# Mamba-2 scan, then PReLU MLP: reordering the first token group (one weight piece ahead of the PReLUs, others behind, states ahead of the scans, later rows moved)

## Chip, cores, metric

One core of one Trainium2 chip. The metric is the device time of one execution in microseconds (us), median over runs. Most runs of one kernel lie within 0.3% of each other, some sets spread more; ranges are given. TensorE is PE, VectorE is DVE, ScalarE is ACT, GpSimd is POOL.

## The reference, cut to what matters

```python
# x (4,8,768,32), a (4,8,768), B, C (4,8,768,16): a chunked state space scan
for c in range(nc):                               # nc = 24 chunks of 32
    L = np.exp(cum[..., :, None] - cum[..., None, :]) * causal
    M = np.einsum('bhin,bhjn->bhij', Cc, Bc) * L
    y = M @ xc + (Cc @ state) * np.exp(cum)[..., None]
    state = decay_full * state + sum_j(B_j x_j decay_from_j)
# then an MLP with a PReLU that has one slope per hidden unit
h = x @ w_in                                      # (3072,256) @ (256,2048)
g = np.maximum(h, 0) + alpha * np.minimum(h, 0)
out = g @ w_out                                   # (2048,256)
```

The weights arrive as 64-bit floats and are made 32-bit on the chip, in 16 pieces of 512 KB (the inputs `in_moe_w_in` and `in_moe_w_out`).

## The kernel before

Tokens go through in six groups of 512 (four chunks of 128, so two pairs of chunks). The first group has a loop of its own over f, the 16 blocks of 128 hidden units: a hidden product, a PReLU, an output product four blocks behind. Between these run the conversion of the weights and the scan (`ssm`) of pairs 2 and 3, which make the second group's tokens.

A piece is converted in six operations: two on ACT and one on POOL (the first part), two on DVE (sign; shift and combine), and a last addition on POOL. The order in which the program issues instructions matters for what an engine waits for: before, ACT's copy of B and C (37.26 us in the timeline that the prediction shows) stands behind the first part of piece 6, which waited for its load until 36.11.

```python
def convert_a(dst, src, sg):                      # first part of a piece
    nc.scalar.activation(out=t, in_=hi, func=ACTF.Abs, scale=0.125)        # ACT
    nc.gpsimd.tensor_scalar(out=t, in0=t, ..., op0=ALU.min, op1=ALU.max)   # POOL, clamp
    nc.scalar.activation(out=g, in_=half, ...)                             # ACT

def convert_b(dst, src, sg):
    nc.vector.tensor_single_scalar(out=r, in_=hi, scalar=SIGN, ...)        # DVE, L238
    nc.vector.scalar_tensor_tensor(out=r, in0=t, scalar=3, in1=r, ...)     # DVE, L239
# convert() adds on POOL (L261); convert_next(first=True) converts the next piece i
# and then issues the first part of piece i + 2

def pair(gp):                                     # each yield ends a stage; gp = 2, 3 here
    ...                                           # transposes of B and C, copy bc
    if not fine:
        spread_c()                                # ACT: two products cz
    bn = bns.pop(gp) if gp in bns else pair_loads(gp)   # POOL: B scaled
    ...
    yield
    decays(0)                                     # DVE: four scans
    yield
    decays(1)                                     # DVE: four scans
    yield
    states(added(ss_tile()))                      # PE: B's products with x; DVE: state
    c_decayed()
    yield
    gram = products_bc()                          # PE: eight score products; one of their four
                                                  # buffers is a hidden-product buffer (two exist)
    ...                                           # DVE: four multiplications, in two stages
    yield
    ...                                           # PE: y; ACT: copy into the next group's tokens

# driver, first group
convert_a(*pieces[3])
prelus = [hidden_two(0, 0, 2 * Q, spare())]       # second-half hidden products of f = 0, 1
prelus[0]()                                       # their PReLUs on DVE
prelus = [hidden_two(0, 2, 2 * Q, spare())]
convert_a(*pieces[4])
convert_next(first=False)                         # piece 3
prelus[0]()
identity_bank()
convert_a(*pieces[5])
convert_next()                                    # piece 4, and first part of piece 6
in_steps = {8: 0, 10: 1, 12: 2, 14: 3}
for f in range(FIRST, NF):                        # f = 4 .. 15
    if f == 9:
        rows_clamp(1); held["pr"] = rows_scan(1); rows_out(1)    # DVE: "the later rows"
    if f <= 10: ssm(2)
    if f >= 9: ssm(3)
    hidden(0, f)                                  # PE, then ACT and DVE for the PReLU
    convert_next()
    output(f - FIRST)                             # PE
    if f in in_steps:
        weight_sums(wi, in_sums, 0, in_steps[f])  # POOL
```

## Time and profile before

| | before |
|---|---|
| time, median of 4 runs | 378.16 us (378.02 to 378.35) |
| span of the profiled run | 376.5 us |
| PE busy, share of span | 365.5 us, 97% |
| PE waits, 26 to 84 us | 3.9 us, all before 62 us |
| transposes of pair 2 to transposes of pair 4 | 30.73 to 85.41 us: 54.68 us |

The last row is the yardstick of this study. Between these two points PE does the same work in every kernel below, and the start of a run is outside it: transposes of pair 2 begin anywhere from 30.1 to 31.0 us without a difference in the program, so whole times carry that noise. The prediction shows the lines of the waits and the timeline.

### The profile page before, as it was taken

What the parts mean: (1) busy time and instruction counts of PE and PEld (TensorE: products, weight loads), DVE (VectorE), ACT (ScalarE), POOL (GpSimd) and SP (SyncE); (2) the same over time, 40 slices, a digit from 0 to 9 for tenths busy, and PEclk for the clock granted to TensorE, in tenths of its full rate; (3) what the DMA queues carried; (4) which work ended last, traced back from release to release, by engine and by line L of the source; (5) the groups of instructions that cost most, each with busy time, mean ns of one, the idle gap of its engine ahead of it and who ended that gap; (6) DMA issues with size and microseconds to landing.
All of it is one profiled execution on the core that took longest, in us unless ns stands there. A gap on an engine that the chain in (4) does not pass through costs nothing.

```text
span 376.5 us, 6178 instructions
## 1 busy us (share of the span) xinstructions
PE 365.5 (97%) x2223; PEld 294.0 (78%) x2223; DVE 242.2 (64%) x461; ACT 179.8 (48%) x384; POOL 203.7 (54%) x212
## 2 busy tenths in 40 slices
PE   8898899999999999999999999999999999999996
PEld 7675466668778788788788788788788788888884
DVE  7885799967537737747737847647856734543364
ACT  2557666525354445445435535535625525543541
POOL 4875366778766836535455445356364355264512
PEclk9999999999999999999999999999999999999999
DMA  7989798821008801001801801901811000001003
GB/s 141 225 190 304 205 276 178 169 67 57 28 0 182 154 2 57 2 0 30 177 6 36 174 2 29 182 0 28 152 33 22 9 0 15 16 0 30 1 0 84
DMA packets 121878, 30.71 MB, mean 82 GB/s; under 512 B 93736, under 2 KB 117752, under 8 KB 121848
## 3 DMA queue, kind: packets, MB, share of 16 engines
q1 hardware_dynamic: 116736, 29.74, 35.6%
q10 hardware_dynamic: 5112, 0.59, 1.1%
q8 instruction: 17, 0.28, 0.3%
q14 instruction: 13, 0.11, 0.1%
HBM read 26.98 MB, written 3.34 MB: 81 GB/s over the span
## 4 chain that ended last, share of the span: by engine, by line
PE 85%; DVE 5%; DMA 3%; POOL 2%; ACT 2%; issue 1%; ACTq 1%; POOLq 0%; DVEq 0%
PE hp L766 33%; PE bank L741 32%; PE bank L680 5%; PE hp L642 3%; PE ss L623 2%; DMA raw<-in_moe_w_in_dram 2%; PE ss L564 2%; PE ss L616 1%; DVE dec L438 1%; PE ss L519 1%; DMA nat<-in_B_dram 1%; PE hp L657 1%; PE hp L564 1%; PE ss L469 1%; DVE wr L239 1%
## 5 line engine op out<-in xcount | busy, mean ns | idle before, releaser
L809 POOL TENSOR_TENSOR gt<-gt 128x512 f32<-128x512 f32 x58 | 73.7, 1271 | 31.7 <-DVE gt L751 24.8
L751 DVE SCALAR_TENSOR_TENSOR gt<-hp,s_mul,gt 128x256 f32<-128x256 f32 x120 | 52.6, 479 | 47.8 <-ACT gt L749 46.8
L741 PE MATMUL bank<-gt,w_out 128*128 128x256 f32 x320 | 82.5, 382 | 0.4 <-ACT o_sb L687 0.4
L749 ACT ACTIVATE gt<-hp,s_alpha 128x256 f32<-128x256 f32 x120 | 50.4, 471 | 47.1 <-PE hp L766 32.8
L741 PEld LDWEIGHTS bank<-gt,w_out 128*128 128x128 f32 x320 | 60.0, 190 | 11.2 <-issue 2.3
L800 POOL TENSOR_TENSOR gt<-gt 128x512 f32<-128x512 f32 x20 | 25.4, 1271 | 78.1 <-DVE gt L751 78.1
L741 PE MATMUL bank<-gt,ws 128*128 128x256 f32 x240 | 58.3, 379 | 0.0
L741 PEld LDWEIGHTS bank<-gt,ws 128*128 128x128 f32 x240 | 45.1, 190 | 5.8
L438 DVE TENSOR_TENSOR_SCAN dec<-abc,bank 128x256 f32<-128x256 f32 x80 | 48.1, 660 | 0.0
L766 PE MATMUL hp<-xs,w_in 128*128 128x256 f32 x160 | 42.8, 390 | 0.0
L766 PE MATMUL hp<-xT,w_in 128*128 128x256 f32 x160 | 41.9, 384 | 0.0
L766 PE MATMUL hp<-xs,ws 128*128 128x256 f32 x160 | 41.1, 379 | 0.0
L785 DVE TENSOR_TENSOR hp<-hp,u 128x512 f32<-128x512 f32 x20 | 14.0, 700 | 39.6 <-ACT u L783 39.6
L774 ACT COPY m<-hp 128x512 f32<-128x512 f32 x20 | 11.7, 586 | 51.4 <-PE hp L766 51.4
L766 PEld LDWEIGHTS hp<-xs,w_in 128*128 128x128 f32 x160 | 28.7, 189 | 7.7 <-issue 3.3
L766 PEld LDWEIGHTS hp<-xs,ws 128*128 128x128 f32 x160 | 30.4, 190 | 4.1
L766 PEld LDWEIGHTS hp<-xT,w_in 128*128 128x128 f32 x160 | 29.7, 190 | 5.0 <-issue 1.4
L680 PEld LDWEIGHTS bank<-w_out,gt 128*128 128x128 f32 x128 | 24.1, 190 | 11.7 <-issue 4.9
L680 PE MATMUL bank<-w_out,gt 128*128 128x256 f32 x128 | 30.7, 381 | 2.3 <-POOL w_out L261 2.3
L789 DVE TENSOR_TENSOR c<-hp,m 128x512 f32<-128x512 f32 x20 | 13.6, 682 | 19.2 <-PE hp L766 19.2
L642 PE MATMUL hp<-xT,w_in 128*128 128x512 f32 x48 | 23.3, 607 | 0.3 <-DVE gt L646 0.3
L783 ACT COPY u<-hp 128x512 f32<-128x512 f32 x20 | 11.7, 586 | 22.9 <-PE hp L766 22.9
(155 smaller groups left out, 553.7 us busy)
## 6 DMA issues: line engine op xcount, KB each, us to landing
abc<-z SPq DMA_DIRECT2D x20, 512.0 KB, 5.3
raw<-in_moe_w_in_dram SPq DMA_DIRECT2D x8, 512.0 KB, 4.9
raw<-in_moe_w_out_dram SPq DMA_DIRECT2D x8, 512.0 KB, 6.5
xt<-in_x_dram SPq DMA_DIRECT2D x24, 128.0 KB, 3.2
out_dram<-o_sb SPq DMA_DIRECT2D x32, 64.0 KB, 1.9
nat<-in_B_dram SPq DMA_DIRECT2D x22, 64.0 KB, 2.8
nat<-in_C_dram SPq DMA_DIRECT2D x22, 64.0 KB, 3.3
ap<-pf SPq DMA_DIRECT2D x11, 128.0 KB
```

Source lines behind the costliest of these rows:

```text
L438: nc.vector.tensor_tensor_scan(out=dv[:, k, hs], data0=abc[k][:, hs], data1=ident_p[0], initial=0.0, op0=ALU.mult, op1=ALU.add)
L642: nc.tensor.matmul(hp, w_in[:, k, f * P : (f + 1) * P], xts[g][:, k], start=(k == 0), stop=(k == KC - 1))
L680: nc.tensor.matmul(pos[0][t // 2][:, t % 2], gt[:, t * Q : (t + 1) * Q], w_out[:, f], start=(f == 0 and t % 2 == 0), stop=(f == NF - 1), s ...
L741: nc.tensor.matmul(ms[g][i][:, h], w, blocks[g, z][n][:, p], start=(q == 0 and h == 0), stop=(q == NQ - 1), skip_group_check=True)
L749: nc.scalar.mul(o[:, p], h[:, p], s_alpha[:, fs[p]])
L751: nc.vector.scalar_tensor_tensor(out=o[:, p], in0=h[:, p], scalar=s_mul[:, fs[p]], in1=o[:, p], op0=ALU.mult, op1=ALU.max)
L766: nc.tensor.matmul(to[:, p], w(2 * z + p), b, start=start and p == 0, stop=True, skip_group_check=True)
L774: nc.scalar.copy(out=m1, in_=A)
L785: nc.vector.tensor_tensor(out=Y, in0=Y, in1=u2, op=ALU.add)
L789: nc.vector.tensor_tensor(out=c22, in0=A, in1=m5, op=ALU.add)
L800: nc.gpsimd.tensor_tensor(out=tc_, in0=g22, in1=g12, op=ALU.subtract)
L809: eng.tensor_tensor(out=o, in0=x0, in1=x1, op=ALU.subtract)
```

## The change

Its intent is to close PE's gaps in the first group: piece 3 ahead of the PReLUs that wait for ACT, the first parts of pieces 5 and 6 behind the PReLU of f=4, B's scaling for pairs 2 and 3 made sooner, their states ahead of the scans (which saves a stage in each), and the later rows from f=9 to f=11.

```diff
 def pair(gp):
-        if not fine:
+        if gp < 2:
             spread_c()
 ...
         else:
+            if gp > 1:
+                states(added(ss_tile()))
+                c_decayed()
             decays(0)
 ...
             if gp != 1:
                 decays(1)
+            if gp > 1:
+                spread_c()
 ...
-            if not fine:
-                yield
-            states(added(ss_tile()))
-            c_decayed()
+            if fine:
+                states(added(ss_tile()))
+                c_decayed()
             yield
             gram = products_bc()
 # driver
     convert_a(*pieces[3])
-    prelus = [hidden_two(0, 0, 2 * Q, spare())]
-    prelus[0]()
-    prelus = [hidden_two(0, 2, 2 * Q, spare())]
+    convert_next(first=False)
+    hidden_two(0, 0, 2 * Q, spare())()
+    rest = hidden_two(0, 2, 2 * Q, spare())
     convert_a(*pieces[4])
+    rest()
+    identity_bank()
+    bns[2] = pair_loads(2)
     convert_next(first=False)
-    prelus[0]()
-    identity_bank()
-    convert_a(*pieces[5])
-    convert_next()
 ...
-        if f == 9:                      # the later rows
 ...
         hidden(0, f)
-        convert_next()
+        if f < FIRST + 2:
+            convert_a(*pieces[f + 1 + (f > FIRST)])
+        convert_next(first=f > FIRST)
+        if f == FIRST:
+            convert_a(*pieces[6])
+        if f == 8:
+            bns[3] = pair_loads(3)
+        if f == 11:                     # the later rows
```

More of the change, by code (lines that the diff above doesn't have):

```diff
@@ L522, in added @@
             return dps
-        if fine:
-            for k in range(2):
-                for w in range(2):
-                    half_decays(k, w)
-                    if k == 1 and w == 1:
-                        spread_c()
-                    yield
-        else:
-            decays(0)
-            if gp == 1:
-                dps = added(dps)
-            if gp:
-                yield
-            if gp != 1:
-                decays(1)
         def states(dps):
@@ L553, in states @@
             masked[b] = st[-1]
+        if fine:
+            for k in range(2):
+                for w in range(2):
+                    half_decays(k, w)
+                    if k == 1 and w == 1:
+                        spread_c()
+                    yield
+        else:
+            if gp > 1:
+                states(added(ss_tile()))
+                c_decayed()
+            decays(0)
+            if gp == 1:
+                dps = added(dps)
+            if gp:
+                yield
+            if gp != 1:
+                decays(1)
+            if gp > 1:
+                spread_c()
         def products_bc():
@@ L590, in pair @@
         else:
-            if not fine:
-                yield
-            states(added(ss_tile()))
-            c_decayed()
+            if fine:
+                states(added(ss_tile()))
+                c_decayed()
             yield
@@ L976 @@
             load_rows(1)
-        if f == 9:
-            rows_clamp(1)
-            held["pr"] = rows_scan(1)
-            rows_out(1)
         if f <= 10:
@@ L985 @@
         hidden(0, f)
-        convert_next()
+        if f < FIRST + 2:
[6 more added lines that the diff above has]
+        if f == 11:
+            rows_clamp(1)
+            held["pr"] = rows_scan(1)
+            rows_out(1)
         output(f - FIRST)
```

## The prediction

> **What bounds the kernel now.** I read the page first: engine shares, then the 40 slices. The TensorE clock is 9 tenths or more in every slice, so the clock is no issue, and PE is busy almost throughout.
>
> ```profile
> PE 365.5 (97%) x2223; PEld 294.0 (78%) x2223; DVE 242.2 (64%) x461; ACT 179.8 (48%) x384; POOL 203.7 (54%) x212
> PE   8898899999999999999999999999999999999996
> ```
>
> Only the first seven slices (9.4 us each) and the last fall short of 9. So a change in the first group of tokens can only win what PE loses there. The second view is PE's waits, once for 26 to 62 us and once for 62 us to the end:
>
> ```profile
> PE bank L680 <- POOL w_out L261: 2.3, 2, 1.4
> PE ss L564 <- DVE state L547: 0.5, 1, 0.5
> PE bank L616 <- DVE dec L600: 0.5, 1, 0.5
> PE hp L642 <- DVE gt L646: 0.3, 1, 0.3
> PE hp L657 <- ACT xT L630: 0.3, 1, 0.3
> ...
> PE bank L741 <- ACT o_sb L687: 0.4, 1, 0.4
> PE turned L852 <- DVE c L878: 0.3, 1, 0.3
> ```
>
> The first five rows are the early stretch, the last two all the rest: 3.9 us against 0.7. After 61 us the chain that ended last is PE work in unbroken order, so a microsecond won before 61 us should come out at the end, provided no new wait arises. The third view is the timeline of 30 to 60 us:
>
> ```profile
> 31.17 1.89 PE L642 MATMUL hp<-xT,w_in 128*128 128x512 f32 x4
> 33.12 1.33 POOL L261 TENSOR_TENSOR w_out<-wr,wg 128x512 uint32<-128x512 uint32 x1
> 33.42 1.57 DVE L239 SCALAR_TENSOR_TENSOR wr<-wt,wr 128x512 uint32<-128x512 uint32 x1
> 34.50 1.99 PE L680 MATMUL bank<-w_out,gt 128*128 128x256 f32 x8 [1.45 <-POOL w_out L261]
> 36.11 0.67 ACT L218 ACTIVATE wt<-raw 128x512 f32<-128x512 f32 x1 [1.33 <-DMA raw<-in_moe_w_in_dram]
> 37.26 0.56 ACT L472 COPY bc<-bank 128x512 f32<-128x512 f32 x1
> 39.37 0.75 DVE L646 SCALAR_TENSOR_TENSOR gt<-hp,s_mul,gt 128x512 f32<-128x512 f32 x1 [4.37 <-ACT gt L645]
> 43.08 1.99 PE L680 MATMUL bank<-w_out,gt 128*128 128x256 f32 x8 [0.86 <-POOL w_out L261]
> 49.19 0.69 DVE L239 SCALAR_TENSOR_TENSOR wr<-wt,wr 128x512 uint32<-128x512 uint32 x1
> 50.19 0.48 PE L564 MATMUL ss<-cz,bc 32*128 32x256 f32 x1 [0.48 <-DVE state L547]
> 59.30 0.34 PE L616 MATMUL bank<-cd,sm 64*128 64x128 f32 x1 [0.45 <-DVE dec L600]
> ```
>
> Two troubles show. The first output product (34.50) waits for weight piece 3, because its conversion on DVE stands behind a PReLU that waits for ACT. And ACT stands still until 36.11 for piece 6 from HBM: behind that first part stand the copy of B and C (37.26), two cz products, and the first full PReLU, for which DVE waits 4.37 us. From 41.6 to 75 us DVE is then busy nearly without a break, working off what it could not do earlier; the later PE waits are its delay.
>
> **What the Trainium skill says.** "SBUF — State Buffer", section "Who interferes with whom": VectorE and GpSimd share one port pair, an exclusive lock; whoever is first holds it for the whole instruction, and a VectorE operation with two SBUF inputs or in a 2-port mode blocks against GpSimd. The trace agrees: L239 (two SBUF inputs) takes 0.69 us with GpSimd idle (49.19) and 1.57 us where GpSimd's addition began just before (33.12, 33.42). The scans L438 and PReLUs L646, with one input in PSUM, stay at 0.66 and 0.74 us. "PSUM — Partial Sum Buffer", section "Engine vs sequencer instructions": ScalarE, VectorE and GpSimd queues are strict FIFO, which is the ACT row at 36.11: work that was ready stood behind one that was not.
>
> **What a gap costs.** A wait costs more than its idle row: a hidden product that follows an output without a wait moves the chain on by 1.72 us, one by itself takes 1.9, so the overlap is lost too. From the start of the hidden product of f=4 (31.17) to that of f=10 (61.03 in the chain) are 29.9 us. The same work at the unhindered steps of the chain after 61 us: six hidden products (1.91 for the four behind a block of other work, 1.72 for f=6 and f=8 behind an output: 11.1), six outputs of 1.73 (10.4), B's products with x 0.4, the eight score products 1.07, y 1.7, four transposes 0.44: 25.1. So 4.8 us is all that can be won. By place: output 0 1.6, hidden 6 0.5, output 2 1.0, score products 1.2, y 0.6 (together 4.9).
>
> **The change part by part.** Instruction counts per engine are unchanged; only the order is.
>
> (1) Piece 3 is converted ahead of the second-half PReLUs. ACT is done with it at 29.0 and GpSimd at 28.9; L239 can run at 28.9 to 29.6, the addition until about 31.0. Output 0 then starts at 32.95, right behind the hidden product: 1.6 us won.
>
> (2) First parts of pieces 5 and 6 go behind the PReLU of f=4. ACT copies B and C at 33.1 (not 37.3), the ACT half of the PReLU runs at 33.7, DVE's half at 34.4 (not 39.4). Hidden 6 no longer waits: 0.5 won. The landing of piece 6 at 36.0 does not move, but only converting work stands behind it. Piece 5 is in w_out by about 38.4 (not 43.0), before output 2 at 40.5: 1.0 won.
>
> (3) B's scaling is ahead (GpSimd at 33.1), the products with x come at f=5, and the state update goes ahead of the scans. The score products find their buffer free: 1.2 won. They also come at f=7 instead of f=8, y at f=9 instead of f=10, for pair 3 at f=14 instead of 15.
>
> (4) The later rows (2.45 us of DVE from 56.0 to 58.5, right ahead of what y waited for) go to f=11: 0.6 won.
>
> What it adds: with a stage less per pair, the same 4.65 us of scans stand closer to the score products, which take one of two hidden-product buffers. So hidden 7 needs the PReLU of f=6. DVE, step by step: L239 of piece 4 is blocked by B's scaling until 33.7, done 34.4; PReLU 4 until 35.0; L238 of piece 5 blocked by the addition of piece 4 until 35.7, done 36.1; L239 behind GpSimd's clamp, 36.4 to 37.1; state 37.4; four scans (2.33) 39.7; PReLU 5 40.3; conversion of piece 6, blocked a little, 41.9; four scans 44.2; PReLU 6 44.9. PE, unhindered, would be there at 43.3 (31.17 + 1.8 + 1.75 + 0.4 + 1.9 + 1.73 + 1.73 + 1.73 + 1.07). A **new wait of 1.7 us**; without the port blocks it would be 0.7. Later, with f=10 starting at time T, DVE does state, scans, PReLU, conversion, scans, PReLU, conversion, rows and the first score multiplication by about T + 12.2, and hidden 13, which needs that multiplication's buffer, could start at T + 11.8: 0.4 lost to the rows.
>
> Sum: 4.8 - 1.7 - 0.4 = 2.7 us; without blocks 4.8 - 0.7 - 0.2 = 3.9. I take 2.9, nearer the first: **378.1 - 2.9 = 375.2 us**.
>
> **Rivals.** *The DVE bound takes it back.* If DVE is the true limit of the first group, the gaps close and reopen at hidden 7 and 13, and only 1 to 1.5 us remain: 376.6 to 377. For it: DVE is 0.89 to 0.98 busy in each 5 us from 40 to 75. Against it: part of that is blocked time, 4.4 us of DVE idle before 39.4 is now used, and per f the plain DVE work (PReLU 0.64, conversion 1.14) is half of PE's 3.45. *The loads are the limit.* Pieces 6 to 10 arrive between 36 and about 40.3 at 320 to 390 GB/s; if ACT, now ahead, runs into piece 7 or 8, the gain of part 2 shrinks: about 376.5. Against it: the first part of piece 7 ran at 39.24 before without a wait, and is wanted at about 38; by rate it lands near 37.5. *All gaps close*: no blocks, 374.0, at the very best 373.3. *Later stages give it back*: they have no PE wait to absorb it and token sums on GpSimd keep some 0.7 us of lead over the product that reads them, so I give this little.
>
> **Range and chances.** The bound of 4.8 us caps the gain at 1.3%, so over 2% faster is nearly excluded; a loss of 2% would need 7.6 us of new waits. Range 374.0 (blocks absent, a little over) to 376.6 (DVE takes back two thirds). Chances: faster 0.01, same 0.98, slower 0.01.
>
> **What would show it.** Right: output 0 starts near 33.0 with no wait for POOL w_out; ACT's wait for piece 6 stands behind the PReLU of f=4; the PE waits on L564's state and L616's dec are gone; a wait of hidden products for the PReLU (DVE gt) of 0.5 to 1.7 us near 43 to 45 us; from there on PE unbroken, y of pair 2 about 7 us earlier. Wrong: output waits on POOL w_out later on, an ACT wait on a raw piece that reaches PE, PE waits past 80 us that were not there, or the hidden wait over 2 us.

## The result, and the profile after

The changed kernel took 377.04 us, median of 4 runs (376.56 to 377.21), against 378.16 us: a ratio of 0.9968, 95% interval 0.9951 to 0.9985. A ratio here is the mean time of one kernel's fast runs over that of the other's of the same rounds, so not quite the ratio of the medians. The gain is about 1.1 us where 2.9 was forecast; 377.04 lies outside the range of 374.0 to 376.6; within 2%, as forecast. All runs counted here and below were in the fast state.

The page of the changed kernel, engine share and slices of PE:

```profile
PE 365.0 (97%) x2223; PEld 294.9 (79%) x2223; DVE 242.4 (65%) x461; ACT 179.1 (48%) x384; POOL 202.1 (54%) x212
PE   8899899899999999999999999999999999999996
```

The fourth slice (28 to 38 us) has risen from 8 to 9, but the eighth (66 to 75 us) has fallen from 9 to 8. PE's waits of the changed kernel from 26 to 84 us (waiter, releaser, us in total, times, longest):

```profile
PE hp L646 <- DVE gt L650: 2.6, 2, 1.6
PE hp L646 <- DVE dec L604: 0.8, 1, 0.8
PE hp L661 <- ACT xT L634: 0.3, 1, 0.3
```

In these rows hp is the buffer of a hidden product, gt the result of a PReLU, dec the decays times the scores, xT the tokens of a group, and bank a buffer of other products.

All the waits that the change aimed at are gone. In their place stand three waits of hidden products, 3.4 us; two of them lie past 62 us, where the kernel before had none. Their places in the timeline of the changed kernel, with output 0 and ACT's wait for piece 6:

```profile
33.13 1.89 PE L684 MATMUL bank<-w_out,gt 128*128 128x256 f32 x8
36.99 0.69 ACT L218 ACTIVATE wt<-raw 128x512 f32<-128x512 f32 x1 [0.92 <-DMA raw<-in_moe_w_in_dram]
45.18 1.98 PE L646 MATMUL hp<-xT,w_in 128*128 128x512 f32 x4 [1.62 <-DVE gt L650]
67.77 1.96 PE L646 MATMUL hp<-xT,w_in 128*128 128x512 f32 x4 [1.00 <-DVE gt L650]
72.22 1.98 PE L646 MATMUL hp<-xT,w_in 128*128 128x512 f32 x4 [0.77 <-DVE dec L604]
```

Output 0 starts at 33.13 behind its hidden product. ACT still waits for piece 6 (until 36.99, where the forecast let it land at 36.0 as before), but nothing on PE's path stands behind it. Hidden 7 (45.18) waits as forecast. Hidden 12 (67.77) and hidden 13 (72.22) are the news. From transposes to transposes it is now 30.97 to 84.28 us: 53.31, so 1.37 won.

What DVE and POOL did ahead of hidden 12, in the timeline of the changed kernel:

```profile
57.72 0.42 DVE L238 TENSOR_SCALAR wr<-raw 128x512 uint32<-128x512 uint32 x1
58.21 1.26 POOL L713 TENSOR_TENSOR ws<-w_in 128x512 f32<-128x512 f32 x1 [2.20 <-DVE wr L238]
58.24 1.79 DVE L239 SCALAR_TENSOR_TENSOR wr<-wt,wr 128x512 uint32<-128x512 uint32 x1
59.95 0.34 DVE L531 SCALAR_TENSOR_TENSOR state<-state,ap,ss 128x128 f32<-128x128 f32 x1
```

POOL's first weight sum writes into the buffer from which L238 reads the raw piece. So it starts just as L238 ends, and that is the moment at which L239 wants to run: 1.79 us instead of 0.69. The state, and all of DVE's work of f=10 and 11 behind it, is 1.1 us late. And ahead of hidden 13 stand the later rows:

```profile
69.21 1.26 POOL L261 TENSOR_TENSOR w_in<-wr,wg 128x512 uint32<-128x512 uint32 x1 [1.16 <-DVE wr L239]
69.30 1.45 DVE L348 TENSOR_TENSOR_SCAN pr<-r,ends 96x128 f32<-96x128 f32 x1
71.48 0.69 DVE L604 TENSOR_TENSOR dec<-hp,dec 128x512 f32<-128x512 f32 x1
```

L348 runs against POOL's addition in the same way (with POOL idle, in experiment 7, the same scan took 0.42 us), and only then comes the multiplication (71.48) that frees the buffer for hidden 13.

### The profile page after: what moved, and what is told of

Its sections match the earlier page's. It is cut to its first block, busy times and chain, and to the rows that moved or that the text cites. A ratio compares the mean times of both kernels' runs of the same rounds, so it can differ in the third digit from the quotient of the medians.

```text
span 375.5 us, 6180 instructions
## 1 busy us (share of the span) xinstructions
PE 365.0 (97%) x2223; PEld 294.9 (79%) x2223; DVE 242.4 (65%) x461; ACT 179.1 (48%) x384; POOL 202.1 (54%) x212
## 4 chain that ended last, share of the span: by engine, by line
PE 86%; DVE 6%; POOL 2%; ACT 2%; issue 1%; POOLq 0%; DVEq 0%; ACTq 0%
PE hp L770 33%; PE bank L745 32%; PE bank L684 4%; PE hp L646 3%; DVE dec L438 2%; PE ss L627 2%; PE hp L661 2%; PE ss L569 2%; PE ss L620 1%; PE ss L469 1%; PE ss L519 1%; PE hp L569 1%; PE hp L270 1%; DVE gt L650 1%; DVE wr L239 1%
```

## The experiments

The theory: the gaps closed by the change are real and worth some 5 us; three new waits eat most of it. They come (A) because a stage less per pair puts the score products, which take one of the two hidden-product buffers, too close behind DVE's scans; (C) at hidden 12, because the weight sum collides with L239; (D) at hidden 13, because of the rows. The rival (B): DVE has no room in the first group, and any reordering only moves the waits.

Summary first; "stretch" is the time between the transposes of pairs 2 and 4, and the waits are PE's from 26 to 84 us without the 0.3 us for xT that all have. The kernel before had medians of 377.62 us (the first four), 378.12 (the next four) and 378.42 (the last) on those chips; the ratio is against it. Medians of different chips don't compare to half a microsecond, and the intervals of 2, 3, 4 and 9 overlap that of the changed kernel: there the stretch and the waits decide, each from one profiled run.

| kernel | waits left, us | stretch, us | median, us (range) | ratio, 95% |
|---|---|---|---|---|
| before | 3.6 | 54.68 | 378.16 | 1 |
| changed | 1.6, 1.0, 0.8 | 53.31 | 377.04 (376.56 to 377.21) | 0.9968 |
| 1: stage back | 0.9 | 50.46 | 374.34 (373.82 to 374.42) | 0.9909 (0.9891 to 0.9927) |
| 2: sums later | 1.6, 0.8 | 52.27 | 375.84 (375.75 to 376.33) | 0.9954 (0.9938 to 0.9970) |
| 3: rows at f=9 | 1.6, 1.0 | 52.29 | 375.68 (375.33 to 377.81) | 0.9952 (0.9932 to 0.9973) |
| 4: both 2 and 3 | 1.6 | 51.25 | 375.06 (374.32 to 376.77) | 0.9938 (0.9915 to 0.9962) |
| 5: stage back, rows at f=14 | none | 49.53 | 373.37 (372.97 to 373.72) | 0.9882 (0.9861 to 0.9903) |
| 6: piece 3 alone, on before | 2.1, 0.8, 0.5, 0.4 | 54.68 | 378.31 (376.76 to 379.00) | 1.0004 (0.9991 to 1.0016) |
| 7: parts 1 and 2, on before | 1.0 | 51.18 | 374.81 (374.40 to 376.25) | 0.9927 (0.9907 to 0.9947) |
| 8: stage back, pair 2 only | 0.8 | 50.54 | 374.33 (374.11 to 375.44) | 0.9917 (0.9898 to 0.9936) |
| 9: B's scaling earlier | 1.4, 1.0, 0.8 | 53.11 | 376.81 (376.49 to 377.42) | 0.9958 (0.9946 to 0.9970) |

### 1. The stage back

```diff
             if gp > 1:
                 spread_c()
+                yield
```

> The changed kernel with one yield put back behind the second half of the scans and the cz products, for pairs 2 and 3: the score products of pair 2 come at f=8 again and those of pair 3 at f=13; all else of the change stays. Theory A (stage theory): the three PE waits of the changed kernel (1.6, 1.0 and 0.8 us, all at hidden products) exist only because the score products, which take one of the two hidden-product buffers, stand one f too close behind the scans; with the stage back all three vanish and no other comes: about 3.4 us of idle and some 0.4 of refill less, 373.3 us (372.9 to 374.2). Rival B (DVE throughput): DVE has no room between 33 and 72 us, so the waits only move to other products: 376.3 to 377.3.

PE's waits of this kernel, 26 to 84 us:

```profile
PE hp L647 <- DVE gt L651: 0.9, 1, 0.9
PE hp L662 <- ACT xT L635: 0.3, 1, 0.3
```

374.34 us, just above the range of theory A (372.9 to 374.2) and far from B. The waits at hidden 7 and 12 are gone, without any DVE work taken away: DVE had room, in other places. One wait is left, at hidden 13, now for the PReLU of f=12, which stands directly behind the rows. So A is right for two waits, not for the third.

### 2. The first weight sums later

```diff
-    in_steps = {8: 0, 10: 1, 12: 2, 14: 3}
+    in_steps = {10: 0, 11: 1, 12: 2, 14: 3}
```

> The changed kernel with the first two weight sums at f=10 and f=11 instead of f=8 and f=10. Theory C (port collision): the first sum starts on GpSimd at the moment the sign operation of f=9 frees its buffer (58.21 us), and the conversion's second operation, two SBUF inputs, then takes 1.79 instead of 0.69 us; it puts all DVE work of f=10 and 11 back by 1.1 us, and this is the 1.0 us wait at hidden 12. Without it: 376.0 us (375.7 to 376.3), no wait at hidden 12, the wait at hidden 13 still there. Theory A alone or B: nothing changes but by noise, 376.8 to 377.3.

In the timeline of this kernel L239 of f=9 and the state behind it:

```profile
57.87 0.69 DVE L239 SCALAR_TENSOR_TENSOR wr<-wt,wr 128x512 uint32<-128x512 uint32 x1
58.58 0.35 DVE L531 SCALAR_TENSOR_TENSOR state<-state,ap,ss 128x128 f32<-128x128 f32 x1
```

0.69 us instead of 1.79, the wait at hidden 12 gone, the stretch shorter by 1.04 us, 375.84 us (theory C said 376.0). The collision is shown: nothing else was moved on DVE.

### 3. The rows back at f=9

```diff
+        if f == 9:
+            rows_clamp(1)
+            held["pr"] = rows_scan(1)
+            rows_out(1)
         if f <= 10:
             ssm(2)
 ...
-        if f == 11:
-            rows_clamp(1)
-            held["pr"] = rows_scan(1)
-            rows_out(1)
```

> The changed kernel with the later rows back at the start of f=9, where DVE stands idle for 3.8 us (53.2 to 57.0). Theory D (rows): the rows at f=11, 2.4 us of DVE of which 1.4 are port blocks, are what hidden 13 waits for (0.8 us); at f=9 they cost nothing: 376.1 us (375.8 to 376.5), the wait at hidden 12 stays. Rival: the rows' load lands too late for f=9 (it was issued at 50.2 behind 1 MB of decays), DVE stands and the PReLU of f=9 is late: 376.8 to 377.6.

The wait at hidden 13 is gone, that at hidden 12 stays, the stretch is shorter by 1.02 us; 375.68 us in the median, a little under the range of theory D (375.8 to 376.5), though one of ten runs took 377.81 at a mean granted clock of 0.995. D holds by the stretch: within the changed kernel, that part of the change is a loss by itself. At f=9, DVE had idled 3.8 us. The two row scans are blocked by POOL at both places (1.45 and 0.76 us at f=11, 1.46 and 0.77 at f=9; 0.42 and 0.40 with POOL idle in experiment 7). So some 1.4 us of what was moved are port blocks, and no run leaves the rows at f=11 without them.

### 4. Sums and rows together

The edits of 2 and 3 together.

> Both: first sums later and rows at f=9. Theories C and D together: both waits of pair 3's score products go, the 1.6 us wait at hidden 7 stays: 375.2 us (374.8 to 375.6). If the two are not independent (DVE's delay is shared), less than the sum of both single gains: 375.7 to 376.2.

The stretch is shorter by 2.06 us, the sum of 1.04 and 1.02: the two are independent. The one wait left (1.6 us) is hidden 7's. The time, 375.06 us, is as expected; two of the six runs took 376.5 and 376.8 at clocks of 0.994 and 0.993, the others 374.3 to 375.2 at 0.998 to 1.

### 5. Stage back, rows at f=14

The edit of 1, and:

```diff
-        if f == 11:                     # the later rows
+        if f == 14:
```

> The changed kernel with the stage back (as in the first experiment) and the later rows at f=14 instead of f=11, behind the last conversion, where DVE had 1.5 us of idle time per f. The one wait that the first experiment left, 0.9 us at hidden 13 for the PReLU of f=12, which stood behind the rows, should go and no other come: 1.0 us less than the first experiment's 374.3, so 373.3 us (372.9 to 373.8) on a chip like that one; from the transposes of pair 2 to those of pair 4 some 49.5 us instead of 50.5. Rival: the granted clock, at 0.993 to 0.999 in some runs with little PE idle, takes it back: 374 us or more with a clock under 1.

PE's waits of this kernel from 14 us to the end:

```profile
PE bank L746 <- ACT o_sb L692: 0.4, 1, 0.4
PE hp L519 <- POOL bn L385: 0.3, 1, 0.3
PE turned L857 <- DVE c L883: 0.3, 1, 0.3
PE hp L662 <- ACT xT L635: 0.3, 1, 0.3
```

None is left in the loop of the first group. The stretch is 49.53 us, 5.15 less than before, and the time 373.37 us, 1.2% under the kernel before: the fastest version of this study. The clock was 0.999 to 1 in all five runs, so the rival did not show here.

### 6. Part 1 alone, on the kernel before

```diff
     convert_a(*pieces[3])
+    convert_next(first=False)
     prelus = [hidden_two(0, 0, 2 * Q, spare())]
     prelus[0]()
     prelus = [hidden_two(0, 2, 2 * Q, spare())]
     convert_a(*pieces[4])
-    convert_next(first=False)
     prelus[0]()
```

> The kernel before with part 1 alone: piece 3 converted ahead of the second-half PReLUs. If each gap of before had its own worth, 1.6 us come: 376.5. My theory now: the next product that waits (hidden 6, for the PReLU of f=4, which stands behind the late piece 6) has its release at the same time as before, so the time won at output 0 is lost again there: output 0 starts at 33.0, hidden 6 at 40.3 as before, and the whole is the same, 377.6 to 378.2.

The first two of PE's waits of this kernel, 26 to 84 us:

```profile
PE hp L642 <- DVE gt L646: 2.1, 1, 2.1
PE bank L680 <- POOL w_out L261: 0.8, 1, 0.8
```

The output wait of 1.4 us is gone, and the wait of hidden 6 has grown from 0.3 to 2.1. Stretch 54.68 us, as before to the last digit, ratio 1.0004. A gap that is closed ahead of a later release is worth nothing by itself.

### 7. Parts 1 and 2 alone, on the kernel before

The driver's edits for pieces 3 to 7 of the change, without the early B scaling, with the stages, the states and the rows of before.

> The kernel before with parts 1 and 2 alone: piece 3 ahead, first parts of pieces 5 and 6 behind the PReLU of f=4; stages of the pairs, B's scaling, the states and the rows as before. Theory: the waits at output 0, hidden 6 and output 2 go (3.1 us), the wait of the score products for the state goes or shrinks, that of y stays or grows (the rows stand ahead of it): 374.3 to 375.3 us, faster than the whole change. Rival: without B's products and states ahead the score products wait as long as before and y takes the rest: 376 or more.

PE's waits of this kernel, 26 to 84 us, without xT's:

```profile
PE bank L616 <- DVE dec L600: 1.0, 1, 1.0
```

This is the only wait: y of pair 2 behind the rows. But DVE itself stood for the load of the rows ahead of them, in the timeline of this kernel:

```profile
53.95 0.43 DVE L339 TENSOR_SCALAR r<-rows 96x128 f32<-96x128 f32 x1 [1.70 <-DMA rows<-in_a_dram]
54.42 0.42 DVE L348 TENSOR_TENSOR_SCAN pr<-r,ends 96x128 f32<-96x128 f32 x1
```

The rows' own work took 1.3 us, the wait for their load 1.70: an earlier load might have spared y's 1.0 us without moving the rows, which no run tests. 374.81 us, stretch 51.18. Two parts of the four make more than the whole change (53.31). The wait of the score products for the state, for which part 3 was made, is gone without part 3.

### 8. The stage back for pair 2 only

```diff
             if gp > 1:
                 spread_c()
+            if gp == 2:
+                yield
```

> The changed kernel with the stage put back for pair 2 only; pair 3 as in the change. If the waits at hidden 7 (pair 2) and at hidden 12 and 13 (pair 3) are independent, only the first goes: 1.9 us less, 375.2, with 1.0 and 0.8 us left. If DVE's lag is carried over from pair 2 to pair 3, PE arrives earlier and waits longer at hidden 12 and 13: 376 to 377. If the lag behind hidden 12 came only from the port collision and shrinks as DVE is ahead, 374.3 to 374.8.

PE's waits of this kernel, 26 to 84 us, without xT's:

```profile
PE hp L648 <- DVE dec L606: 0.8, 1, 0.8
```

The waits at hidden 7 and at hidden 12 go both; hidden 13's stays; stretch 50.54. Independent waits would have given 1.9 us; 2.8 came, within the third of the forecasts but not quite for its reason: L239 of f=9 still collides (1.81 us in its timeline). With y of pair 2 at f=10 again, PE has that block's work between hidden 9 and hidden 12, which gives DVE the time that the collision takes; that is how I read the two timelines, no run tests it apart. The collision then costs only where DVE has nothing to spare.

### 9. B's scaling of pair 2 earlier

```diff
     rest = hidden_two(0, 2, 2 * Q, spare())
+    bns[2] = pair_loads(2)
     convert_a(*pieces[4])
     rest()
     identity_bank()
-    bns[2] = pair_loads(2)
     convert_next(first=False)
```

> The changed kernel with B's scaling for pair 2 put ahead of piece 4's first part, where GpSimd stood idle (31.3 to 32.65 us), instead of behind it. The prediction said that port blocks make 1.0 of the 1.7 us wait at hidden 7, one of them the conversion operation of piece 4 held by B's scaling (0.94 instead of 0.69 us in the changed kernel, the following addition 0.25 later too). If the blocks add up along the chain to the PReLU of f=6, the wait shrinks by 0.25 to 0.5 us: 1.1 to 1.4 instead of 1.6, and the time by the same, 376.6 to 376.8, too little to tell by the time alone; the wait in the profile decides. If DVE's later waits for GpSimd and ACT swallow it, 1.6 stays.

From the timeline of this kernel, the conversion of piece 4 on DVE and hidden 7 on PE:

```profile
33.64 0.69 DVE L239 SCALAR_TENSOR_TENSOR wr<-wt,wr 128x512 uint32<-128x512 uint32 x1
44.93 1.98 PE L646 MATMUL hp<-xT,w_in 128*128 128x512 f32 x4 [1.40 <-DVE gt L650]
```

The operation that took 0.94 us with B's scaling beside it takes 0.69, and the wait at hidden 7, eleven microseconds later, is 1.40 instead of 1.62. One port block of 0.25 us goes through the chain nearly whole. The time (376.81) can't tell it. The other blocks on that chain were not taken away, so how much of the 1.6 us they make in all stays open.

## Why the prediction was wrong

The mechanism was right in its parts, and the size of one term of the sum was off.

- **What can be won** (4.8 us). Right, a little low: the kernel without loop waits has a stretch of 49.53 us, 5.15 less than before.
- **Parts 1, 2 and 3 close the early gaps.** Right: no wait of the earlier list is left in the changed kernel but xT's. But the worths by place (1.6, 0.5, 1.0, 1.2, 0.6) don't stand alone: part 1 alone is worth nothing (experiment 6), and part 3 wasn't needed for its own gap (experiment 7).
- **The new wait at hidden 7** (1.7 us). Right: 1.62 us, for the PReLU of f=6, and it goes with the stage (experiment 8).
- **The second term, "0.4 lost to the rows".** This is the failed step. It measured 1.8 us of waiting, and 2.06 in the stretch (experiment 4): 1.04 for a collision at hidden 12, where the forecast had no wait at all, and 1.02 for the rows with their own port blocks. The forecast let DVE reach the first score multiplication of pair 3 by T + 12.2, T being the start of hidden 10. With T = 58.54 that is done by 70.7 in the forecast and was done at 72.17. Of the 1.4 us between, 1.1 is the blocked L239 of f=9; in the timeline L238 of f=10 and of f=11 took 0.67 and 0.79 us where 0.42 is free, another 0.6 (part of which the sum had). The forecast had charged 1.0 us of port blocks up to hidden 7 and only 0.2 from there on, too little for L239 of f=9.
- **What speaks against me.** The block stood in the timeline of before, at the same step:

```profile
60.83 1.27 POOL L709 TENSOR_TENSOR ws<-w_in 128x512 f32<-128x512 f32 x1 [2.67 <-DVE wr L238]
60.85 1.79 DVE L239 SCALAR_TENSOR_TENSOR wr<-wt,wr 128x512 uint32<-128x512 uint32 x1
```

  It cost nothing there, as PE came later to the products that depend on it. I took durations from free rows of the kind (0.69) and not from the row of the very instruction (1.79). With the 1.1 us of that row added, 4.8 - 1.7 - 1.5 = 1.6 us would have been forecast; with the 1.8 that were measured, 1.3.
- **Part 4, the rows.** The 0.6 us ahead of y were credited, and 0.4 charged at hidden 13. In the changed kernel the multiplications for y are done by 51.0 us, and between the conversion at 52.6 and the PReLU of f=9 DVE then idles 3.8 us; so the rows at f=9 had cost nothing, and the move itself lost 1.02 us (experiment 3). With before's stages (experiment 7) y waits 1.0 us behind the rows at f=9, but there DVE had stood 1.70 us for their load, so that wait may be the load's and not the place's. At f=14 the rows cost no wait with the stages of before (experiment 5).
- **Small slips.** The slices of before that fall short of 9 are the first, second, fourth, fifth and last, not all of the first seven. Piece 6 did land later, by 0.9 us. Neither had weight in the sum.
- **Rivals.** "The DVE bound takes it back" came nearest in time (376.6 to 377) and is wrong as a cause: experiment 5 does the same DVE work with no wait. Loads and later stages took nothing.

What stays open: in how far single blocks make the 1.6 us at hidden 7, how much of the 1.02 us of the rows is their port blocks, and why whole times of one kernel spread by 2 us in some sets (376.76 to 379.00 in experiment 6).

## What to carry to other kernels

Once one wait is closed, go on along the same chain to the next release and ask whether it moved too; the first gap alone may be worth nothing. When work is put a stage earlier, list what it takes from the loop (here one of two buffers) and follow the slower engine to that point, with the durations of those very instructions in the trace, blocked ones included. A block that costs nothing today stands ready on the path of a faster schedule; and the move of a side task (the rows) has to be judged in the new order, not in the old. Before a wait is put down to such a task, look whether the task itself waited for its load.

## What the Trainium skill lacked or had wrong

- "SBUF — State Buffer", section "Who interferes with whom", agrees with the rows looked at here: L239 with two SBUF inputs 0.69 us alone and 1.79 beside a POOL addition that began 0.03 us earlier; L238 0.42 alone and, in the changed kernel, up to 1.09; a row scan with two SBUF inputs 1.45 us beside a POOL addition that began 0.09 us earlier, and 0.42 with POOL idle (experiment 7).
- "Perfetto Trace Analysis", section "Per-instruction lifecycle: what the profiler-reported window actually captures", names no wait for this port in VectorE's window. In these traces the block lies inside the reported duration (1.79 us for L239, no idle time ahead), so a blocked DVE looks busy. From 63 to 68 us of the changed kernel it reads 4.90 of 5 us busy, of which L238 has 0.67 and 0.79 us where 0.42 is free.
- No page read for this study says that a buffer's release can line up two engines: the weight sum waits for L238 of the piece whose buffer it takes, and so meets L239 within 0.03 us in every kernel that has it at f=8 (1.79 to 1.81 us in nine traces: before, changed, experiments 1, 3 and 5 to 9).
